# Attention in front of two expert layers: scores and values on four quadrants of TensorE, scores in two PSUM banks, v loaded by even and odd heads

## The chip, the cores and the metric

The kernel runs on one core of one Trainium2 chip. The metric is the device time of one execution in microseconds; before the change the median of two timed runs is 1208.76 us (1208.47 to 1209.05). The profile is one further execution of the same program, recorded by the hardware profiler.

## The reference

Attention inside chunks of 64 tokens, then a gated layer with a root-mean-square norm, then four weighted expert layers, all in float32 (the weights of the gated and the expert layers arrive as float64):

```python
# q, k, v: (4, 8, 576, 64): batch, heads, tokens, head size
q_c, k_c, v_c = (a.reshape(B, H, nc, 64, D) for a in (q, k, v))
scores = np.matmul(q_c, k_c.transpose(0, 1, 2, 4, 3)) / np.sqrt(D)
scores = scores - np.max(scores, axis=-1, keepdims=True)
attn = np.exp(scores)
attn = attn / (np.sum(attn, axis=-1, keepdims=True) + 1e-09)
out = np.matmul(attn, v_c)

x = out.transpose(0, 2, 1, 3).reshape(2304, 512)
xn = x / np.sqrt(np.mean(x * x, axis=-1, keepdims=True) + 1e-06) * rms_g
g = xn @ w_gate                      # 512 x 1536
x = (g / (1 + np.exp(-g)) * (xn @ w_val)) @ w_out

p = probs / (probs.sum(-1, keepdims=True) + 1e-09)
out = sum(p[:, e:e+1] * (np.maximum(x @ w1[e], 0) @ w2[e]) for e in range(4))
```

## The kernel before

The 2304 tokens are cut into 18 tiles of 128 tokens (two chunks of 64) and into five blocks (four of 512 tokens, one of 256). The attention goes tile by tile and fills, for each block, the transposed and normed input of the gated layer in two parts (`xh` and `xl`, the rounded value and what the rounding left). Once a block's tiles are there, the first gate and value units (matmuls `gps` and `vps`, 128x512, line 1170) can run; they are what TensorE has to do beside the attention. Everything after that is large matmuls of 256 or 512 columns.

One tile of the attention, in `attention` (from line 548 on), with the names that the profile shows:

- SP loads q, k and v, each as 128 tokens x 8 heads x 64 (`load_qkv`, line 516; a tile that crosses from one batch to the next takes two DMAs). There are two buffers each for q and k, three for v.
- TensorE transposes q and k, four 128x128 transposes each (`tps`, line 553). ScalarE or VectorE copies them to `qT` and `kT` (lines 562, 564), where 64 rows hold an even head and 64 rows an odd one.
- TensorE computes the scores, 16 products of 64x64 (`sc`, line 583). Head `r` of a pair stands on rows `r * 64` on, and its result goes to the same partitions: rows and result are both `r`. Each product of two float32 operands is two matmuls in the trace, so a tile has 32.
- VectorE takes the maximum and subtracts it (`mx`, line 602; `e`, line 607), ScalarE takes the exponent (line 620; from tile 8 on for two tiles at once).
- TensorE transposes again (`eps`, line 629), an engine copies to `eT` (lines 642, 644), and TensorE multiplies by v, 16 products of 64x65 (`xps`, line 658); the column behind the 64 holds ones, so the row sums come with it. Here both the rows and the result are the chunk `c`.
- VectorE adds up and divides (`den`, `xs`, lines 670 to 676). ScalarE squares (`junk`, line 690), GpSimd takes the root (line 700), GpSimd or VectorE applies the gain (line 707) and ScalarE or VectorE the scale (lines 712, 714).
- TensorE transposes the result (`xtps`, line 723); ScalarE writes `xh` and a plain copy `xf` (lines 731, 744), VectorE writes `xl` (line 736).

PSUM has eight banks: four for the transposes and the scores of the attention (tags `y0` to `y3`, resource "a"), two for the gate and value units (`h0`, `h1`), and one pair of two for the values (tag `av`). When the attention is over, the banks pass to the later stages.

The order of the work on each engine is not written by hand. Class `Plan` is given every step with its engine or engines, an assumed cost, what it needs, which buffers it takes and gives back, and a rank; it lists the steps by the earliest start, walks backwards over the result to set new ranks, repeats this with some random changes up to 120 times and emits the order of the best pass. So a changed cost or a changed number of buffers moves instructions on all engines. Each engine then works through its own queue in order. Line numbers here and in the profile are those of the kernel before.

Of the kernel before, what the change touches and what calls it, by code (L numbers as in the profile page):

```python
# [10 lines left out]
F32 = mybir.dt.float32  # L11
# [4 lines left out]
ALU = mybir.AluOpType  # L16
# [209 lines left out]
def tile_attention_moe_moe2(  # L226
# [135 lines left out]
    plan.buffers("a", [f"y{d}" for d in range(KD)])  # L362
    plan.buffers("av", ["av"])
# [45 lines left out]
    def h_bank(tag, n, name):  # L409
        p = ps_y if tag[0] == "y" else ps_h if tag[1] != "x" else opened()["h"]  # L410
        return p.tile([P, n], F32, tag=tag, name=name)
# [96 lines left out]
    def load_qkv(nm, i):  # L508
        def emit(_, tag):
            src = {"q": q, "k": k, "v": v}[nm]  # L510
            if nm == "v":
                t = v_tiles[tag]
            else:
                t = at_p.tile([P, H, D], F32, tag=tag, name=nm)
# [17 lines left out]
    def attention(grp):  # L532
# [10 lines left out]
        for i in grp:  # L543
# [31 lines left out]
            def scores(_, tag, etag=None, i=i):  # L575
                qT, kT = tiles.pop(("qT", i)), tiles.pop(("kT", i))
                sc = a_bank(tag, [P, HP, 2, CH], "sc")
                for hp in range(HP):
                    for c in range(2):
                        for r in range(2):  # L580
# [3 lines left out]
                                out=sc[rows, hp, c, :], lhsT=qT[rows, hp, cols], rhs=kT[rows, hp, cols],  # L584
                                start=True, stop=True,
                            )
                tiles["sc", i] = sc.rearrange("p a c k -> p (a c) k")
# [3 lines left out]
            s2 = add("PE", 1.2, scores, needs=[cp["q"], cp["k"]], takes=["a"] + (["e"] if i == key else []), rank=rank(i, 16))  # L591
# [8 lines left out]
            def maximum(_, i=i):  # L600
                mx = sm_p.tile([P, H, 1], F32, tag="mx", name="mx")
# [3 lines left out]
            def subtract(_, i=i):  # L605
                o = (i - key) * H
                nc.vector.tensor_tensor(
                    out=tiles["ee", key][:, o:o + H, :], in0=tiles.pop(("sc", i)),
                    in1=tiles.pop(("mx", i)).to_broadcast([P, H, CH]), op=ALU.subtract,
# [4 lines left out]
            sub.gives.append(("a", s2, 0))  # L614
# [9 lines left out]
        for n_, i in enumerate(grp):  # L624
# [25 lines left out]
            def values(_, tag, xtag, i=i):  # L650
                eT, vv = tiles.pop(("eT", i)), tiles.pop(("v", i))
                ps = ps_a.tile([P, 2, 512], F32, tag=tag, name="xps")
                ps = ps[:, :, 0:HP * VW].rearrange("p b (h e) -> p b h e", e=VW)
                for h in range(H):
                    hp, r = h // 2, h % 2
                    for c in range(2):
                        rows = slice(c * CH, (c + 1) * CH)
                        nc.tensor.matmul(  # L658
                            out=ps[rows, h // HP, h % HP, 0:D + 1], lhsT=eT[rows, hp, r * CH:(r + 1) * CH],
                            rhs=vv[rows, h, 0:D + 1], start=True, stop=True,  # L660
                        )
                tiles["xps", i] = ps

            s4 = add("PE", 1.2, values, needs=[ce, first[i]["v"]], takes=["av", "xs"], rank=rank(i, 8))
# [9 lines left out]
            def divide(_, i=i, s4=s4):  # L674
                xs = xs_tiles[s4.ids[1]][:, 0:DM]
                nc.vector.tensor_tensor(
                    out=xs.rearrange("p (b h d) -> p b h d", b=2, h=HP), in0=tiles.pop(("xps", i))[:, :, :, 0:D],
# [1697 lines left out]
```

## Time and profile before

| what | value |
|---|---|
| median of the timed runs | 1208.76 us |
| the profiled execution: span from the first to the last instruction | 1891.7 us |
| mean granted TensorE clock in it | 0.587 |
| TensorE busy (PE) | 1885.1 us |
| VectorE busy (DVE) | 953.0 us |
| ScalarE busy (ACT) | 609.1 us |
| GpSimd busy (POOL) | 251.7 us |
| moved to and from HBM | 235.66 MB |

The profiled execution is much longer than the timed ones. Its span is the only time that is known of it; what lies around the span (the start and the end of an execution) is in no row. The clock column (PEclk) gives the share of full speed (2.4 GHz) that TensorE was granted; its two levels are 1.2 and 2.4 GHz. Engines other than TensorE do not depend on that clock. PEld is TensorE's loading of weights, which overlaps its matmuls. Idle time of an engine that is not the bottleneck costs nothing.

### The profile page before, as it was taken

What the parts mean: (1) busy time and instruction counts of PE and PEld (TensorE: products, weight loads), DVE (VectorE), ACT (ScalarE), POOL (GpSimd) and SP (SyncE); (2) the same over time, 40 slices, a digit from 0 to 9 for tenths busy, and PEclk for the clock granted to TensorE, in tenths of its full rate; (3) what the DMA queues carried; (4) which work ended last, traced back from release to release, by engine and by line L of the source; (5) the groups of instructions that cost most, each with busy time, mean ns of one, the idle gap of its engine ahead of it and who ended that gap; (6) DMA issues with size and microseconds to landing.
All of it is one profiled execution on the core that took longest, in us unless ns stands there. A gap on an engine that the chain in (4) does not pass through costs nothing.

```text
span 1891.7 us, 18628 instructions
## 1 busy us (share of the span) xinstructions
PE 1885.1 (100%) x6962; PEld 1244.2 (66%) x6962; DVE 953.0 (50%) x1407; ACT 609.1 (32%) x957; POOL 251.7 (13%) x198
## 2 busy tenths in 40 slices
PE   9999999999999999999999999999999999999999
PEld 7876666566566665666666666766776666666666
DVE  4655454455456355554545455454656344444455
ACT  5554223332334332323323232232332322222222
POOL 1331110111211001010112112121200011110110
PEclk5555555555555555555555555555666666666666
DMA  8631233324233423333522424243354433534333
GB/s 178 136 69 51 67 112 138 112 85 171 90 139 111 145 89 122 124 132 112 183 105 107 160 96 150 78 150 123 112 178 154 160 130 129 167 138 140 122 111 107
DMA packets 161967, 235.66 MB, mean 125 GB/s; under 512 B 67213, under 2 KB 103125, under 8 KB 161877
## 3 DMA queue, kind: packets, MB, share of 16 engines
q1 hardware_dynamic: 161876, 234.47, 37.7%
q8 instruction: 55, 0.90, 0.2%
q14 instruction: 36, 0.29, 0.0%
HBM read 145.53 MB, written 88.90 MB: 124 GB/s over the span
## 4 chain that ended last, share of the span: by engine, by line
PE 100%; ACT 0%; issue 0%; POOL 0%; DVE 0%; POOLq 0%; ACTq 0%
PE yps L1905 35%; PE hps L1713 25%; PE hps L1316 17%; PE hps L2176 4%; PE yr L2220 4%; PE hps L1445 2%; PE vps L1170 2%; PE gps L1170 2%; PE xps L658 2%; PE tps L553 2%; PE sc L583 2%; PE yo L1523 1%; PE eps L629 1%; PE xtps L723 1%; PE ot L2088 1%; PE warm L2265 0%
## 5 line engine op out<-in xcount | busy, mean ns | idle before, releaser
L1905 PE MATMUL yps<-ha,w 128*128 128x512 f32 x1860 | 667.2, 541 | 0.0
L1905 PEld LDWEIGHTS yps<-ha,w 128*128 128x128 f32 x1860 | 395.9, 215 | 257.2 <-issue 123.1
L1713 PE MATMUL hps<-xa,w 128*128 128x512 f32 x1344 | 479.1, 535 | 0.0
L1713 PEld LDWEIGHTS hps<-xa,w 128*128 128x128 f32 x1344 | 285.6, 215 | 173.6 <-issue 75.2
L1832 DVE TENSOR_TENSOR ha<-hs,ha 128x1024 fp32r<-128x1024 f32 (+1 forms) x126 | 139.5, 1119 | 103.9 <-ACT ha L1826 103.8
L1826 ACT ACTIVATE ha<-hs 128x1024 fp32r<-128x1024 f32 (+1 forms) x126 | 119.0, 959 | 185.6 <-PE yps L1905 140.7
L1937 DVE TENSOR_TENSOR acc<-acc,yps 128x512 f32<-128x512 f32 (+1 forms) x130 | 87.8, 678 | 116.8 <-PE yps L1905 116.4
L1849 POOL TENSOR_TENSOR hs<-hs 128x1024 f32<-128x1024 f32 (+1 forms) x32 | 69.7, 2178 | 517.5 <-DVE ha L1832 487.8
L955 ACT ACTIVATE w<-raw 128x512 fp32r<-128x512 f32 x127 | 77.7, 627 | 120.7 <-PE hps L1713 48.0
L1726 ACT ACTIVATE hps<-hps 128x512 f32<-128x512 f32 x64 | 37.2, 582 | 232.9 <-PE hps L1713 232.9
L1316 PE MATMUL hps<-xh,w 128*128 128x512 f32 x216 | 109.8, 575 | 0.0
L1316 PE MATMUL hps<-xs,w 128*128 128x512 f32 x264 | 106.7, 577 | 0.0
L962 POOL TENSOR_TENSOR w<-raw,w 128x512 fp32r<-128x512 f32 x38 | 52.9, 1394 | 340.6 <-ACT w L955 269.3
L1920 ACT ACTIVATE yps<-yps 128x512 f32<-128x512 f32 x88 | 51.2, 581 | 118.0 <-PE yps L1905 116.2
L1774 DVE SCALAR_TENSOR_TENSOR hs<-hps,pb 128x512 f32<-128x512 f32 x96 | 65.5, 687 | 42.5 <-PE hps L1713 42.4
L1316 PEld LDWEIGHTS hps<-xs,w 128*128 128x128 f32 x264 | 58.0, 220 | 43.5 <-issue 24.6
L962 DVE TENSOR_TENSOR w<-raw,w 128x512 fp32r<-128x512 f32 x89 | 65.2, 754 | 36.6 <-ACT w L955 36.4
L1734 DVE TENSOR_TENSOR hps<-hps,p 128x512 f32<-128x512 f32 x32 | 22.4, 699 | 116.3 <-ACT hps L1726 116.3
L1832 DVE TENSOR_TENSOR ha<-hl,ha 128x1024 fp32r<-128x1024 f32 x42 | 50.8, 1224 | 52.2 <-ACT ha L1826 52.2
L2220 PEld LDWEIGHTS yr<-w,hb 128*128 128x128 f32 x384 | 72.7, 259 | 5.2 <-issue 2.3
L2176 PE MATMUL hps<-xh,w 128*128 128x256 f32 x256 | 75.1, 374 | 0.0
L2220 PE MATMUL yr<-w,hb 128*128 128x256 f32 x384 | 74.1, 373 | 0.0
(175 smaller groups left out, 2126.4 us busy)
## 6 DMA issues: line engine op xcount, KB each, us to landing
w<-wk SPq DMA_DIRECT2D x126, 512.0 KB, 4.1
wk<-w SPq DMA_DIRECT2D x111, 512.0 KB, 3.0
raw<-in_moe_w_dram SPq DMA_DIRECT2D x33, 512.0 KB, 4.6
hl<-sd SPq DMA_DIRECT2D x48, 256.0 KB, 3.1
sd<-s SPq DMA_DIRECT2D x38, 256.0 KB, 2.2
w<-wk SPq DMA_DIRECT2D x32, 256.0 KB, 2.9
wk<-w SPq DMA_DIRECT2D x29, 256.0 KB, 2.0
raw<-in_moe_w_gate_dram SPq DMA_DIRECT2D x12, 512.0 KB, 3.7
```

The costliest lines, as they stand in the source:

```text
L955: nc.scalar.activation(out=w1t[key, c][:, :, 0], in_=half(c in "DA"), func=AF.Copy)
L962: e_.tensor_tensor(out=w[:, :, 1], in0=half(c in "DA"), in1=f32(w[:, :, 0]), op=ALU.subtract)
L1170: nc.tensor.matmul(out=banks[u], lhsT=w[:, wi, kk, :], rhs=x[j][:, kk, 0:n], start=(kk, p) == (0, 0), stop=(kk, p) == (KD - 1, 2),)
L1316: nc.tensor.matmul(out=bank[b], lhsT=w[:, m, wi, kk, :], rhs=xx[xi][:, kk, :], start=start and (kk, i) == (0, 0), stop=(kk, i) == (1, 2), ...
L1713: nc.tensor.matmul(out=bank[b], lhsT=w[:, m, wi, kk, :], rhs=xx[xi][:, kk, :], start=start and (kk, i) == (0, 0), stop=(kk, i) == (1, 2), ...
L1826: nc.scalar.activation(out=ops[tg, g][m][0][:, cuts[k]], in_=x(frm, k), func=AF.Copy)
L1832: nc.vector.tensor_tensor(out=l[:, cuts[k]], in0=x(frm, k), in1=f32(h[:, cuts[k]]), op=ALU.subtract)
L1849: e_.tensor_tensor(out=x(to, k), in0=x(one, k), in1=x(two, k), op=op)
L1905: nc.tensor.matmul(out=bank[b, d][:, cols], lhsT=w[:, m, wi, d, :], rhs=hh[xi][:, fp, cols], start=start and (fp, i) == (0, 0), stop=(fp, ...
L1937: nc.vector.tensor_tensor(out=a[:, cols], in0=a[:, cols], in1=bank[b, d][:, cols], op=ALU.subtract if minus else ALU.add)
L2176: nc.tensor.matmul(out=got["b"], lhsT=w[:, m, wi, kk, :], rhs=(xh, xl)[xi][REST][:, 2 * m + kk, 0:n], start=(m, kk, k) == (0, 0, 0), stop= ...
L2220: nc.tensor.matmul(out=got["y"][:, d * 2 * P:(d + 1) * 2 * P], lhsT=hs[2 * g + f // 2][:, f % 2, xi, t * P:(t + 1) * P], rhs=w[:, f % 2, w ...
```

## The change

Scores and values now use all four 64x64 quadrants of TensorE's array: a head or key half `r` on the rows, and the chunk `c` on the columns, so the result of chunk `c` stands on partitions `c * 64` on. Two row halves that write the same partitions write to different PSUM banks: the scores of even heads go to one bank, of odd heads to another. So the scores now take a pair of banks, as the values do. There are two such pairs (`av0`, `av1`), and two banks instead of four are left for transposes (`y0`, `y1`). For the values, the rows of v must hold even heads on the lower 64 partitions and odd heads on the upper ones, so a tile of v is loaded by four DMAs (two chunks, two halves of the heads) of 64 partitions each. VectorE's steps follow the new layout of the scores and of the values. The assumed cost of scores and values goes from 1.2 to 0.6.

```diff
-    plan.buffers("a", [f"y{d}" for d in range(KD)])
-    plan.buffers("av", ["av"])
+    plan.buffers("a", ["y0", "y1"])
+    plan.buffers("av", ["av0", "av1"])
...
     def h_bank(tag, n, name):
-        p = ps_y if tag[0] == "y" else ps_h if tag[1] != "x" else opened()["h"]
+        p = ps_y if tag in ("y0", "y1") else ps_h if tag in ("h0", "h1") else opened()["h"]
...
             if nm == "v":
                 t = v_tiles[tag]
-            else:
-                t = at_p.tile([P, H, D], F32, tag=tag, name=nm)
+                for off, n, b, s in runs(i * P, P):
+                    for c in range(n // CH):
+                        for r in range(2):
+                            nc.sync.dma_start(
+                                out=t[r * CH:(r + 1) * CH, off // CH + c, :, 0:D],
+                                in_=src[b, r::2, s + c * CH:s + (c + 1) * CH, :].rearrange("h p d -> p h d"),
+                            )
+                tiles[nm, i] = t
+                return
+            t = at_p.tile([P, H, D], F32, tag=tag, name=nm)
...
-                sc = a_bank(tag, [P, HP, 2, CH], "sc")
+                sc = ps_a.tile([P, 2, 512], F32, tag=tag, name="sc")
+                sc = sc[:, :, 0:HP * CH].rearrange("p r (h k) -> p r h k", k=CH)
                 for hp in range(HP):
                     for c in range(2):
                         for r in range(2):
                             rows = slice(r * CH, (r + 1) * CH)
                             cols = slice(c * CH, (c + 1) * CH)
                             nc.tensor.matmul(
-                                out=sc[rows, hp, c, :], lhsT=qT[rows, hp, cols], rhs=kT[rows, hp, cols],
+                                out=sc[cols, r, hp, :], lhsT=qT[rows, hp, cols], rhs=kT[rows, hp, cols],
                                 start=True, stop=True,
                             )
...
-            s2 = add("PE", 1.2, scores, needs=[cp["q"], cp["k"]], takes=["a"] + (["e"] if i == key else []), rank=rank(i, 16))
+            s2 = add("PE", 0.6, scores, needs=[cp["q"], cp["k"]], takes=["av"] + (["e"] if i == key else []), rank=rank(i, 16))
...
-                    out=tiles["ee", key][:, o:o + H, :], in0=tiles.pop(("sc", i)),
-                    in1=tiles.pop(("mx", i)).to_broadcast([P, H, CH]), op=ALU.subtract,
+                    out=tiles["ee", key][:, o:o + H, :].rearrange("p (h r) k -> p r h k", r=2),
+                    in0=tiles.pop(("sc", i)), in1=tiles.pop(("mx", i)).to_broadcast([P, 2, HP, CH]), op=ALU.subtract,
...
-                ps = ps[:, :, 0:HP * VW].rearrange("p b (h e) -> p b h e", e=VW)
-                for h in range(H):
-                    hp, r = h // 2, h % 2
+                ps = ps[:, :, 0:HP * VW].rearrange("p r (h e) -> p r h e", e=VW)
+                for hp in range(HP):
                     for c in range(2):
-                        rows = slice(c * CH, (c + 1) * CH)
-                        nc.tensor.matmul(
-                            out=ps[rows, h // HP, h % HP, 0:D + 1], lhsT=eT[rows, hp, r * CH:(r + 1) * CH],
-                            rhs=vv[rows, h, 0:D + 1], start=True, stop=True,
-                        )
+                        for r in range(2):
+                            rows = slice(r * CH, (r + 1) * CH)
+                            cols = slice(c * CH, (c + 1) * CH)
+                            nc.tensor.matmul(
+                                out=ps[cols, r, hp, 0:D + 1], lhsT=eT[rows, hp, cols],
+                                rhs=vv[rows, c, hp, 0:D + 1], start=True, stop=True,
+                            )
...
-            s4 = add("PE", 1.2, values, needs=[ce, first[i]["v"]], takes=["av", "xs"], rank=rank(i, 8))
+            s4 = add("PE", 0.6, values, needs=[ce, first[i]["v"]], takes=["av", "xs"], rank=rank(i, 8))
...
-                    out=xs.rearrange("p (b h d) -> p b h d", b=2, h=HP), in0=tiles.pop(("xps", i))[:, :, :, 0:D],
+                    out=xs.rearrange("p (h r d) -> p r h d", r=2, h=HP), in0=tiles.pop(("xps", i))[:, :, :, 0:D],
```

The planner's new order shows on every engine; the last 4181 of TensorE's 6388 instructions stand as before, while on the engines beside it steps trade places, and some change between VectorE, ScalarE and GpSimd, up to the last few dozen instructions. On TensorE, before, where the first gate unit comes in between the tiles of the attention (a product of two float32 operands counts once here, so a set of scores is x16):

```order
L583 MATMUL sc<-kT,qT 64x64 x16
L629 MATMUL eps<-ident,e 128x128 x4
L553 MATMUL tps<-ident,q 128x128 x4
L553 MATMUL tps<-ident,k 128x128 x4
L1170 MATMUL gps<-xh_93,w 128x512
L1170 MATMUL gps<-xl_98,w 128x512
L1170 MATMUL gps<-xh_93,w 128x512 x2
L1170 MATMUL gps<-xl_98,w 128x512
L1170 MATMUL gps<-xh_93,w 128x512
L723 MATMUL xtps<-ident,xs 128x128 x4
```

On TensorE, after the change, at the same place (lines have moved by nine or ten):

```order
L592 MATMUL sc<-kT,qT 64x64 x16
L561 MATMUL tps<-ident,q 128x128 x4
L1180 MATMUL gps<-xh_93,w 128x512
L1180 MATMUL gps<-xl_98,w 128x512
L1180 MATMUL gps<-xh_93,w 128x512 x2
L1180 MATMUL gps<-xl_98,w 128x512
L1180 MATMUL gps<-xh_93,w 128x512
L638 MATMUL eps<-ident,e 128x128 x4
L561 MATMUL tps<-ident,k 128x128 x4
```

With two banks, k's transposes no longer follow q's; gate matmuls and the transposes of e stand between them.

On SP, which issues the loads, before, where the loads of the first weights (`raw`) come in between those of the tiles:

```order
L516 DMA q<-in_q_dram 128x8x64
L779 DMA raw<-in_moe_w_gate_dram 128x4x256
L516 DMA k<-in_k_dram 128x8x64
L516 DMA v<-in_v_dram 128x8x64
L516 DMA q<-in_q_dram 128x8x64
L779 DMA raw<-in_moe_w_val_dram 128x4x256
L516 DMA k<-in_k_dram 128x8x64
L516 DMA v<-in_v_dram 64x8x64 x2
```

On SP, after the change, in the same stretch:

```order
L789 DMA raw<-in_moe_w_val_dram 128x4x256
L524 DMA q<-in_q_dram 128x8x64
L516 DMA v<-in_v_dram 64x4x64 x8
L789 DMA raw<-in_moe_w_gate_dram 128x4x256
L524 DMA k<-in_k_dram 128x8x64
L516 DMA v<-in_v_dram 64x4x64 x8
L524 DMA q<-in_q_dram 128x8x64
```

Each tile of v is four DMAs instead of one or two, here for two tiles in a row (x8), and a load of k or q stands behind them. In all there are 72 loads of v instead of 20.

## Rows read from the trace of the kernel before

**Rows 1.** The cores: span, and mean granted TensorE clock.

```profile
core 0: 1891.7 us, clock 0.587
```

**Rows 2.** The page: busy time by engine, and the granted clock in 40 slices.

```profile
PE 1885.1 (100%) x6962; PEld 1244.2 (66%) x6962; DVE 953.0 (50%) x1407; ACT 609.1 (32%) x957; POOL 251.7 (13%) x198
...
PEclk5555555555555555555555555555666666666666
```

**Rows 3.** Busy time by stage: stretch, length, engines, granted clock, DMA share, GB/s.

```profile
core 0: us, PE busy (x) PEld busy (x) DVE busy (x) ACT busy (x) POOL busy (x), PEclk, DMA share, GB/s
0.00:130.00 130.00, 127.17 (x1349) 100.66 (x1350) 70.93 (x132) 68.06 (x124) 34.04 (x44) 0.57 0.63 137
130.00:300.00 170.00, 170.00 (x619) 108.77 (x618) 85.98 (x146) 62.49 (x107) 30.66 (x30) 0.56 0.25 86
300.00:1302.00 1002.00, 1002.00 (x3075) 648.63 (x3074) 501.58 (x738) 316.82 (x492) 135.05 (x95) 0.56 0.35 121
```

**Rows 4.** The chain of waits, 47 to 53 us: start, us, what.

```profile
47.34 0.71 PE xtps L723 x4
48.05 1.67 PE xps L658 x32
49.72 0.86 PE eps L629 x4
50.58 1.66 PE sc L583 x32
52.24 0.86 PE xtps L723 x4
```

**Rows 5.** The first scores of one block: stretch, length, matmuls and weight loads under way.

```profile
43.95:43.95 0.01, 0.01 (x2) 0.01 (x2) 0.56 0.00 0
43.96:44.05 0.09, 0.09 (x2) 0.09 (x4) 0.56 0.00 0
44.05:44.06 0.01, 0.01 (x4) 0.01 (x5) 0.56 0.00 0
44.06:44.11 0.05, 0.05 (x4) 0.05 (x6) 0.56 0.00 0
44.11:44.12 0.01, 0.01 (x6) 0.01 (x5) 0.56 0.00 0
```

**Rows 6.** Groups by line, VectorE, 0 to 260 us: division and subtraction.

```profile
L676 DVE TENSOR_TENSOR xs<-xps,den 128x512 f32<-128x512 f32 x18 | 12.4, 690 | 0.6
L607 DVE TENSOR_TENSOR e<-sc,mx 128x512 f32<-128x512 f32 x18 | 12.4, 687 | 0.6
```

**Rows 7.** The timeline, 28.6 to 34 us: transposes and their last evictions.

```profile
28.63 0.93 PE L553 MATMUL tps<-ident,q 128*128 128x128 f32 x4
...
29.31 0.96 PE L553 MATMUL tps<-ident,k 128*128 128x128 f32 x4
...
29.66 0.60 ACT L562 ACTIVATE qT<-tps 128x512 f32<-128x512 f32 x1 [1.38 <-PE tps L553]
...
30.11 0.97 PE L629 MATMUL eps<-ident,e 128*128 128x128 f32 x4
...
30.38 0.69 DVE L564 COPY kT<-tps 128x512 f32<-128x512 f32 x1 [0.15 <-PE tps L553]
...
30.92 0.87 PE L723 MATMUL xtps<-ident,xs 128*128 128x128 f32 x4
...
31.11 0.60 ACT L642 ACTIVATE eT<-eps 128x512 f32<-128x512 f32 x1 [0.24 <-PE eps L629]
...
33.23 0.69 DVE L736 TENSOR_TENSOR xl<-xtps,xh 128x512 fp32r<-128x512 f32 x1 [1.77 <-ACT xf L744]
```

**Rows 8.** SP: the loads of v (duration min/median/max), and what its queue waited for.

```profile
L516 SPq DMA_DIRECT2D v<-in_v_dram x20: 367/588/2750, 7.2 to 133.2; - x20
...
SPq L516 <- PE tps L553: 46.7, 21, 6.6
SPq L516 <- PE xps L658: 19.9, 4, 9.8
```

More of the change, by code (lines that the diff above doesn't have):

```diff
@@ L583, in scores @@
                             nc.tensor.matmul(
-                                out=sc[rows, hp, c, :], lhsT=qT[rows, hp, cols], rhs=kT[rows, hp, cols],
+                                out=sc[cols, r, hp, :], lhsT=qT[rows, hp, cols], rhs=kT[rows, hp, cols],
                                 start=True, stop=True,
                             )
-                tiles["sc", i] = sc.rearrange("p a c k -> p (a c) k")
+                tiles["sc", i] = sc
                 if i == key:
                     tiles["ee", i] = at_p.tile([P, ng * H, CH], F32, tag=etag, name="e")
-            s2 = add("PE", 1.2, scores, needs=[cp["q"], cp["k"]], takes=["a"] + (["e"] if i == key else []), rank=rank(i, 16))
+            s2 = add("PE", 0.6, scores, needs=[cp["q"], cp["k"]], takes=["av"] + (["e"] if i == key else []), rank=rank(i, 16))
             s2.gives += [("qT", norm["q", i], 1), ("kT", norm["k", i], 1)]
@@ L600, in maximum @@
             def maximum(_, i=i):
-                mx = sm_p.tile([P, H, 1], F32, tag="mx", name="mx")
+                mx = sm_p.tile([P, 2, HP, 1], F32, tag="mx", name="mx")
                 nc.vector.tensor_reduce(out=mx, in_=tiles["sc", i], axis=AX.X, op=ALU.max)
@@ L613, in attention @@
             sub = add("DVE", 0.69, subtract, needs=[m], rank=rank(i, 14))
-            sub.gives.append(("a", s2, 0))
+            sub.gives.append(("av", s2, 0))
             subs.append(sub)
@@ L2255, in tile_attention_moe_moe2 @@
         for i in range(3):
-            t = v_tiles[f"v_{i}"] = at_p.tile([P, H, VW], F32, tag=f"v_{i}", name="v")
-            nc.gpsimd.memset(t[:, :, D:VW], 1.0)
+            t = v_tiles[f"v_{i}"] = at_p.tile([P, 2, HP, VW], F32, tag=f"v_{i}", name="v")
+            nc.gpsimd.memset(t[:, :, :, D:VW], 1.0)
         for i in range(2):
```

## The prediction

> **What bounds the kernel now.** I read the cores first [rows 1], then the page's busy times and clock row [rows 2], the busy times by stage [rows 3], the chain of waits in a settled part of the attention [rows 4], single matmuls in it [rows 5], and last the evictions, transposes and loads that the change touches [rows 6 to 8].
>
> The profiled execution has a span of 1891.7 us, and the timed ones have a median of 1208.76 us. The rows show why these differ: in the profile TensorE was granted 0.587 of full speed on the mean [rows 1], nearer to its lower level (1.2 GHz) than to its upper (2.4 GHz), and was busy for 1885.1 of the 1891.7 us [rows 2]. At full clock that is about 0.587 x 1891.7 = 1110 us of TensorE work. A timed run of 1208.76 us must therefore have had at least 1110 / 1208.76 = 0.92 of the clock. The other engines' busy times do not hang on TensorE's clock. So a stage that reads as "PE 100%" here may belong to another engine in a timed run, and each stage has to be worked out again: TensorE's busy time times its clock, beside the others as they stand.
>
> For the attention, 0 to 130 us [rows 3], that gives TensorE 127.2 x 0.57 = 72.5 us, VectorE 70.9, ScalarE 68.1, and the DMA engines a busy share of 0.63 x 130 = 81.9. Four resources need nearly the same, and TensorE is not the largest. For 130 to 300 us it gives TensorE 170 x 0.56 = 95.2 against VectorE 86.0, and for 300 to 1302 us 561 against 501.6: there TensorE leads. The change touches only the first stage.
>
> **The change part by part.** Sum, in the profile's own time: one block of scores takes 1.66 us and one of values 1.67 [rows 4]. There are 18 of each: 18 x (1.66 + 1.67) = 59.9 us. In these blocks matmuls begin two at a time: two are in flight until 44.05, four from there, six from 44.11 [rows 5]. The code writes only the quadrants (0,0) and (1,1), so two quadrants work beside each other. After the change every quadruple of instructions goes to four quadrants. If those work as independently as the two do, a block takes half: 59.9 / 2 = 29.9 us less TensorE time, 1.6% of the span. At the clock of that stage this is 29.9 x 0.56 = 16.8 us at full clock, and at the 0.92 of the timed runs 16.8 / 0.92 = 18.2 us. The number of matmuls and loads is unchanged. Bounds: nothing, if the two new quadrants do not overlap, and 16.8 to 18.2 us, if TensorE bounds the stage throughout.
>
> What of that lies on the path? With 16.8 us taken off, TensorE needs 72.5 - 16.8 = 55.7 us in a stage where VectorE needs 70.9, ScalarE 68.1 and the DMA engines 81.9. Nothing of what these three do gets less. What remains is that a tile's work passes from engine to engine, and each tile spends less time in its scores and values before the next engine may start. Between 0 and 16.8 I take a third, 5.6 us: nearer to zero, since three resources each need more than TensorE will. TensorE's tail of the program is ordered as before (its last 4181 of 6388 instructions); on the engines beside it steps trade places there, which may go either way by a few us and is left to the range.
>
> The maximum, the subtraction and the division keep their 512 elements. Subtraction now writes pieces of 64 elements, and both read two banks. The division before already reads pieces from two banks and takes 690 ns, the plain subtraction 687 [rows 6]: 36 x 3 ns is 0.1 us. I take zero.
>
> Four banks for transposes become two. A tile has four sets of transposes, each holding a bank until its last eviction ends [rows 7]: q from 28.63 to 29.66 + 0.60 = 1.63 us, k from 29.31 to 31.07 = 1.76, e from 30.11 to 31.71 = 1.60, x from 30.92 to 33.92 = 3.00. That is 7.99 us per tile, over two banks 4.0 us, over 18 tiles 71.9 us. In a timed run the four transposes of a set are quicker (about 0.80 us here, 0.80 x 0.56 = 0.45 there), so 7.99 - 4 x 0.35 = 6.6 us, 59 us in all. That fits beside the 81.9 of the DMA engines, so I cost it at nothing. The cover is gone once evictions wait longer (third rival). The order shows the planner living with it: k's transposes no longer follow q's directly but stand behind gate matmuls.
>
> Loads of v go from 20 to 72 on SP. A v issue takes 0.367 to 2.750 us, median 0.588 [rows 8]. 52 more are 52 x 0.367 = 19.1 us at the minimum and 30.6 us at the median. SP's queue is in order, and the loads of q and k behind v in it are delayed by 3 x 0.37 to 3 x 0.59, or 1.1 to 1.8 us per tile. What hides this is that SP waits for TensorE to free q and k buffers: 46.7 us, and 19.9 us for v's [rows 8]. That cover is 66.6 us in the profile and less in a timed run. Bounds 0 to 30.6 us. I take zero, since the cover is more than twice the median cost.
>
> Sum: -5.6 us, 1208.76 - 5.6 = 1203 us.
>
> A rule of the Trainium skill speaks against the change and is weighed here. In the trace, four weight loads are already under way while the first two matmuls run, before the second pair begins [rows 5], and before the change there are only two quadrants that those loads can go to. So a load runs beside the matmul of its own row group. "TensorE: Matmul & The Clock Gate", Part 3 (the mechanism), says that a weight load overlaps matmuls in flight only when the row groups differ. By that rule the two quadrants of one row half would take turns after the change, a block would not get shorter, and the sum would be 1208.8. The trace does not bear the rule out here, so it gets a small share of the second rival.
>
> **The rivals.**
>
> First: TensorE bounds the attention in timed runs too, because its clock there is not full (0.92 is only the mean). For it: no other engine is seen to hold TensorE in the profile, where its idle time in 130 us is 2.8 us [rows 3]. Against it: at 0.92 TensorE needs 72.5 / 0.92 = 78.8 us, still under the 81.9 of DMA. Time: 1208.8 - 17 or 18 = 1191.
>
> Second: nothing comes of it, because the stage ends with loads and evictions, or because four quadrants do not overlap (the rule above). For it: DMA's 81.9 is the largest need of the stage. Against it: DMA's share counts packets in flight, and goes over what moves. Time: 1208.
>
> Third, slower: two banks. The mechanism is TensorE's in-order queue. The first transpose of a set waits for an eviction, and behind it stand scores, values and gate matmuls that could run; VectorE and ScalarE then wait for those. Without any wait the banks need 59 us of the stage's 81.9. It decides once a set holds its bank longer by (81.9 x 2 / 18 - 6.6) / 4 = 0.6 us, which is one instruction of VectorE (0.69) in front of each eviction. With two in front, 1.38 us, a tile needs 6.6 + 4 x 1.38 = 12.1 us, the stage 18 x 12.1 / 2 = 109 us, 27 us more than 81.9. Between one (3 us) and two (27 us) I price it at 12 us: 1221. For it: VectorE and ScalarE are nearly full in this stage. Against it: two banks of their own now serve scores and values, which took turns with the transposes before.
>
> **How the numbers follow.** The forecast (a part of the saving, 1196 to 1207) gets 0.45, TensorE-bound (about 1191) 0.25, nothing (about 1208) 0.15, slower by the banks or by SP (about 1221) 0.15. The time is that of the likeliest, 1203. For 8 in 10 the range takes in most of the first rival and the nearer half of the third: 1189 to 1217. A change of over 2% is 24 us, about what a measurement of this kernel can tell from none. Faster by that means under 1184.6, more than the whole saving of 18.2 us: 0.05. Slower by that means over 1232.9, reached only with nearly two instructions in front of every eviction, or with all 30.6 us of SP showing: 0.04. Within: 0.91.
>
> **What would show it.** In the changed kernel's chain of waits a block of 32 scores or values should read about 0.83 us at a granted clock of 0.56 (0.47 us at full clock) instead of 1.66, with matmuls beginning four at a time. If it reads 1.6, the second rival's quadrants are right. VectorE's and ScalarE's busy times in the attention should be as before. TensorE's idle time should grow there, ended by evictions if the third rival is right, and by loads if SP is late. If the profile is taken at a low clock again, its span should shrink by up to 1.6%, and by more of it than the timed runs show; timed runs that shrink by as much would mean that the stage was TensorE's after all.

## The result, and the profile after

The changed kernel takes 1223.62 us (median; 1223.49 to 1223.76) against 1208.76. The ratio is 1.0121, 95% interval 1.0091 to 1.0150: slower by 1.2%, or about 14.6 us, where 1203 was forecast and the range ended at 1217.

The profile shown ahead of the prediction had a granted clock of 0.587 [rows 1]. The kernel before was profiled again (run before_again) and was then granted 0.999 (1.000 is full speed), as every later profile was granted 0.987 or more; it is this second profile that the one after can be laid beside. The page of before, profiled again (busy time, clock in 40 slices):

```profile
PE 1194.0 (99%) x6962; PEld 1015.3 (84%) x6962; DVE 956.1 (79%) x1407; ACT 601.6 (50%) x957; POOL 248.9 (21%) x198
```

and of the changed kernel:

```profile
PE 1186.1 (97%) x6962; PEld 1003.8 (82%) x6962; DVE 963.1 (79%) x1411; ACT 603.8 (49%) x960; POOL 240.0 (20%) x191
...
PEclk9899899999999999999999999999999999999999
```

TensorE is busy for 7.9 us less, yet the span went from 1208.5 to 1221.6 us: 21 us of idle time came in. VectorE's and ScalarE's busy times are as before within 1%. The clock row dips in its second and fifth slice only (a slice is 30.5 us, so both lie in the first 153 us). By stretches of 20 us, the kernel before (columns as in [rows 3]):

```profile
0.00:20.00 20.00, 15.09 (x223) 13.38 (x224) 6.45 (x11) 8.67 (x15) 1.27 (x14) 1.00 0.99 184
20.00:40.00 20.00, 16.69 (x278) 14.02 (x277) 14.68 (x30) 14.56 (x28) 6.48 (x7) 0.91 0.93 211
40.00:60.00 20.00, 18.10 (x319) 15.72 (x319) 18.01 (x35) 15.82 (x30) 8.48 (x9) 1.00 0.91 195
60.00:80.00 20.00, 19.83 (x297) 17.06 (x294) 18.16 (x33) 15.74 (x31) 9.22 (x9) 1.00 0.98 208
80.00:100.00 20.00, 20.00 (x298) 17.40 (x297) 17.04 (x34) 17.21 (x29) 11.22 (x10) 1.00 0.51 106
...
120.00:140.00 20.00, 20.00 (x105) 17.09 (x104) 18.45 (x22) 11.82 (x16) 2.63 (x3) 1.00 0.14 54
...
0.00:140.00 140.00, 129.71 (x1682) 111.21 (x1683) 111.68 (x193) 98.13 (x172) 50.38 (x60) 0.99 0.68 150
```

and the changed one:

```profile
0.00:20.00 20.00, 14.52 (x227) 12.51 (x228) 6.92 (x12) 8.60 (x15) 1.28 (x14) 1.00 0.83 167
20.00:40.00 20.00, 11.28 (x201) 9.19 (x200) 13.46 (x26) 11.49 (x21) 0.90 (x2) 0.83 0.92 200
40.00:60.00 20.00, 12.20 (x309) 9.71 (x307) 17.43 (x35) 15.54 (x32) 9.73 (x10) 1.00 0.81 169
60.00:80.00 20.00, 17.12 (x264) 13.93 (x265) 11.87 (x25) 12.42 (x22) 6.78 (x7) 0.91 0.77 164
80.00:100.00 20.00, 18.78 (x281) 15.32 (x280) 17.57 (x31) 16.43 (x31) 10.22 (x8) 1.00 0.78 162
...
120.00:140.00 20.00, 15.29 (x90) 11.64 (x89) 17.68 (x30) 12.19 (x22) 8.03 (x7) 0.84 0.27 90
...
0.00:140.00 140.00, 108.94 (x1612) 88.16 (x1613) 102.20 (x188) 92.91 (x168) 44.24 (x55) 0.94 0.68 150
```

The difference lies in the first 140 us. In these TensorE did 129.7 x 0.99 = 128.4 us of full-clock work before and 108.9 x 0.94 = 102.4 now. The change takes 15.1 us of work away (below), so 128.4 - 15.1 - 102.4 = 10.9 us are late at 140 us, most of the 13.1 us by which the spans differ. Two things read differently as well: the loads moved 164 to 200 GB/s in the first 80 us, where they moved 184 to 211 before, and go on at 162 GB/s from 80 to 100 us; and a new hole of 4.7 us, with a lower clock, opens at 120 to 140 us.

The blocks themselves got shorter nearly as forecast. From the chain of waits, before profiled again:

```profile
71.61 1.08 PE sc L583 x32
...
73.71 1.08 PE xps L658 x32
```

and after:

```profile
67.66 0.63 PE xps L668 x32
...
78.98 0.69 PE sc L592 x32
```

18 x (1.08 + 1.08 - 0.69 - 0.63) = 15.1 us less TensorE work, where 16.8 was forecast. Two sizes behind that were off and nearly cancel: a block went to 0.6 of its time, not to half, and at full clock it took 1.08 us before, not 1.66 x 0.56 = 0.93.

What TensorE waits for in the first 140 us (us in total, times, longest) was, before:

```profile
PE tps L553 <- DMA k<-in_k_dram: 3.4, 4, 1.7
PE tps L553 <- ACT e L620: 2.4, 1, 2.4
```

and after:

```profile
PE xtps L733 <- ACT xs L722: 9.7, 3, 7.4
PE tps L561 <- DVE raw L817: 5.1, 1, 5.1
...
PE tps L561 <- DMA q<-in_q_dram: 2.5, 2, 1.6
PE gps L1180 <- DVE xl L746: 2.1, 1, 2.1
PE tps L561 <- DMA k<-in_k_dram: 1.9, 3, 0.9
```

The largest, xtps behind xs (9.7 us), is a place in TensorE's order: transposes of x stand ahead of work that could run. The 5.1 us are put down to a conversion of VectorE (`raw`), which writes nothing that the transposes of q read; the trace shows what they waited for. The load of q that SP issued at 55.54 us told of its landing at 61.96 us, and the transposes began at 62.10. In SP's queue that load stood behind eight quarter loads of v, which took SP 6.25 us from 48.55 us on. So the waits for loads of q and k come to 2.5 + 1.9 + 5.1 = 9.5 us, where before had 3.4 and, by the same reading, the 2.4 us put down to `e`.

### The profile page after: what moved, and what is told of

It is laid out like the page before. It is cut to its first block, busy times and chain, and to the rows that moved or that the text cites. A ratio compares the mean times of both kernels' runs of the same rounds, so it can differ in the third digit from the quotient of the medians.

```text
span 1221.6 us, 18708 instructions
## 1 busy us (share of the span) xinstructions
PE 1186.1 (97%) x6962; PEld 1003.8 (82%) x6962; DVE 963.1 (79%) x1411; ACT 603.8 (49%) x960; POOL 240.0 (20%) x191
## 4 chain that ended last, share of the span: by engine, by line
PE 92%; DVE 3%; DMA 2%; ACT 1%; issue 1%; POOL 0%; SPq 0%; DVEq 0%; POOLq 0%; ACTq 0%
PE yps L1915 34%; PE hps L1723 25%; PE hps L1326 15%; PE yr L2230 4%; PE hps L2186 4%; PE hps L1455 2%; PE gps L1180 2%; PE yo L1533 1%; PE tps L561 1%; PE vps L1180 1%; PE xps L668 1%; DMA k<-in_k_dram 1%; PE sc L592 1%; DMA g_bc<-in_moe_rms_g_dram 1%; PE ot L2098 1%
## 5 line engine op out<-in xcount | busy, mean ns | idle before, releaser
L1915 PE MATMUL yps<-ha,w 128*128 128x512 f32 x1860 | 425.9, 388 | 0.0
L1915 PEld LDWEIGHTS yps<-ha,w 128*128 128x128 f32 x1860 | 346.3, 188 | 70.4
L1723 PE MATMUL hps<-xa,w 128*128 128x512 f32 x1344 | 313.2, 390 | 0.0
L1723 PEld LDWEIGHTS hps<-xa,w 128*128 128x128 f32 x1344 | 250.2, 188 | 50.7 <-DVE p L1747 0.2
L1326 PE MATMUL hps<-xh,w 128*128 128x512 f32 x232 | 77.5, 389 | 0.0
L1326 PE MATMUL hps<-xs,w 128*128 128x512 f32 x264 | 65.3, 390 | 0.1
L1326 PEld LDWEIGHTS hps<-xs,w 128*128 128x128 f32 x264 | 49.3, 188 | 10.9 <-ACT hps L1340 0.5
L979 DVE TENSOR_TENSOR raw<-raw 128x256 f32<-128x256 f32 x113 | 48.0, 425 | 12.9 <-POOL w L972 7.7
L1836 ACT ACTIVATE ha<-hl 128x1024 fp32r<-128x1024 f32 x42 | 43.7, 1056 | 21.7 <-PE yps L1915 11.7
L1326 PEld LDWEIGHTS hps<-xh,w 128*128 128x128 f32 x232 | 43.6, 188 | 8.9
```

Source lines behind the costliest of these rows:

```text
L1326: nc.tensor.matmul(out=bank[b], lhsT=w[:, m, wi, kk, :], rhs=xx[xi][:, kk, :], start=start and (kk, i) == (0, 0), stop=(kk, i) == (1, 2), ...
L1723: nc.tensor.matmul(out=bank[b], lhsT=w[:, m, wi, kk, :], rhs=xx[xi][:, kk, :], start=start and (kk, i) == (0, 0), stop=(kk, i) == (1, 2), ...
L1836: nc.scalar.activation(out=ops[tg, g][m][0][:, cuts[k]], in_=x(frm, k), func=AF.Copy)
L1915: nc.tensor.matmul(out=bank[b, d][:, cols], lhsT=w[:, m, wi, d, :], rhs=hh[xi][:, fp, cols], start=start and (fp, i) == (0, 0), stop=(fp, ...
```

## The experiments

The change has four parts that can be taken apart: the banks, the quadrants, v's four loads a tile, and the 0.6 us (for 1.2) at which scores and values are booked in the planner, which sets the order of all engines. The theory after the result: the quadrants gain what was forecast, and v's loads or the new order cost more. The rival: the two banks (third rival of the prediction). A third idea was a single load, g_bc (the gain row), that the new order issues late. Ratios are to the kernel before, with their 95% intervals.

**First batch** (the kernel before beside it: 1209.64 us).

before_again asks which engine bounded the attention at full clock:

> The kernel before, unchanged, for a profile at the clock of the timed runs. If TensorE has about 10 us of idle time in its attention here (its work at full clock, some 1195 us, is nearly the whole span), TensorE bounded that stage after all and the four-quadrant saving was there to be had. If it idles 20 us or more, other engines bounded it as the prediction said. Time 1208 to 1210.

1210.3 us. TensorE's idle time in the first 140 us is 140 - 129.7 = 10.3 us, the first case of the expectation: TensorE bounded that stage, and the saving was there to be had. c12_v_one, below, shows how much of it.

v_one, against the changed kernel (it leaves out v's new layout, so it does the same work but doesn't compute the reference):

```diff
-                    for c in range(n // CH):
-                        for r in range(2):
-                            nc.sync.dma_start(
-                                out=t[r * CH:(r + 1) * CH, off // CH + c, :, 0:D],
...
+                    nc.sync.dma_start(
+                        out=t.rearrange("p c h e -> p (c h) e")[off:off + n, :, 0:D],
+                        in_=src[b, :, s:s + n, :].rearrange("h p d -> p h d"),
+                    )
```

> The changed kernel with its order kept, but v loaded by one or two DMAs per tile in the old layout, so that the values multiply rows of v that belong to other heads (the amount of work is the same, the output is not the reference's). SP theory: the four loads of v take 2.6 to 3.5 us of SP's queue per tile in place of 0.6, and q, k and the gain row wait behind them; without them the time falls to 1193 to 1204. Bank theory: two banks for transposes hold TensorE; the time stays at 1217 to 1224.

1216.16 us, ratio 1.0052 [1.0037, 1.0067]. That lies between the ranges of the two theories. The four loads cost about 0.7%, somewhat over half of the loss; the rest stays with v loaded whole.

g_early, the changed kernel with g_bc's load issued right behind the third load of k:

> The changed kernel with the load of the gain row issued right behind the k of the third tile, all else in the same order. In the changed kernel TensorE waits 7.4 us for the first scaled tile, behind that load. If that wait is a loss of its own, the time falls by 5 to 8 us, to 1216 to 1219. If SP's queue holds the stage anyway (SP theory), the wait only moves to the next load: 1220 to 1224.

1223.86 us, 1.0118 [1.0103, 1.0133]: no gain. One late load is not the cause.

b_banks, the kernel before with the changed one's banks:

```diff
-    plan.buffers("a", [f"y{d}" for d in range(KD)])
-    plan.buffers("av", ["av"])
+    plan.buffers("a", ["y0", "y1"])
+    plan.buffers("av", ["av0", "av1"])
...
-            s2 = add("PE", 1.2, scores, needs=[cp["q"], cp["k"]], takes=["a"] + ...
+            s2 = add("PE", 1.2, scores, needs=[cp["q"], cp["k"]], takes=["av"] + ...
```

> The kernel before with only its banks changed: two for transposes, two pairs for scores and values, scores on two quadrants as before, v in one or two DMAs; the planner orders it anew. Bank theory: slower than before by 8 us or more, 1217 or above. SP theory: within 4 us of before, 1205 to 1213.

1213.14 us, 1.0024 [1.0008, 1.0041]. The banks, with the order that the planner makes for them, cost some 3 us, a fifth of the loss, and not the 8 us or more of the bank theory. How much of the 3 us is the banks' and how much the draw of a new order is not shown: c12 and c12_seed6, below, differ by 0.18% in nothing but the draw.

**Second batch** (before: 1208.6 us): the changed kernel with the booking put back,

```diff
-            s2 = add("PE", 0.6, scores, ...
+            s2 = add("PE", 1.2, scores, ...
...
-            s4 = add("PE", 0.6, values, ...
+            s4 = add("PE", 1.2, values, ...
```

with v in four loads (c12), and with v_one's edit as well (c12_v_one).

> The changed kernel with the planner told 1.2 for scores and values as before, so that its order is that of b_banks, and v in one or two DMAs in the old layout (the values multiply rows of v of other heads; the work is the same). Against b_banks (1213.1) only the four quadrants are new. If TensorE bounds the attention, all of the 16 us shows: 1197 to 1200. If loads and VectorE bound it, as the prediction said, little shows: 1206 to 1213.

1206.02 us, 0.9974 [0.9962, 0.9986]: faster than the kernel before, but like v_one it doesn't compute the reference. The order on every engine is that of b_banks, so the step from there is the quadrants (with VectorE's new layout) alone: -0.50%, or -6 us. The first 140 us of b_banks and of c12_v_one:

```profile
0.00:140.00 140.00, 130.56 (x1665) 110.22 (x1666) 107.40 (x192) 102.85 (x181) 40.71 (x54) 0.98 0.69 152
```

```profile
0.00:140.00 140.00, 124.83 (x1705) 100.72 (x1706) 113.25 (x199) 106.92 (x188) 42.07 (x55) 0.95 0.71 159
```

With shorter blocks TensorE's idle time rises from 9.4 to 15.2 us and its granted clock falls from 0.98 to 0.95: part of the 15.1 us goes into waiting for others and into the clock.

> The changed kernel with the planner told 1.2 for scores and values, v in four DMAs as in the change. Against c12_v_one only the loads of v differ. SP theory: they cost 7 us or more here too, 1208 to 1222, c12_v_one plus 7 to 12. If the cost of the loads hung on the planner's order for 0.6, the two differ by less than 3 us.

1215.02 us, 1.0043 [1.0026, 1.0060]. The four loads cost 0.69% here too (from c12_v_one), and the booking 0.78% (from c12 to the changed kernel). The first of these shows in what TensorE waits for in the first 140 us. In c12:

```profile
PE tps L561 <- DMA k<-in_k_dram: 4.8, 4, 2.4
PE tps L561 <- DMA q<-in_q_dram: 4.5, 3, 2.5
```

and in c12_v_one, with the same order:

```profile
PE tps L559 <- DMA k<-in_k_dram: 2.0, 1, 2.0
```

One more wait in each (3.3 and 2.0 us) is put down to another engine, but there too the load had landed 0.14 us before the transposes began, as in the others. With these it is 12.6 us against 4.0: 8.6 us more, beside 8.3 us of time. The changed kernel has 9.5 us of such waits and v_one 0.8. With seed 6 (fourth batch) the waits at 0.6 differ by as much, those at 1.2 only by about 4 us.

> The changed kernel with its order, v in one or two DMAs in the old layout, and the gain row loaded behind the third k. In v_one TensorE still waits 6.7 us for the first scaled tile behind the gain row. If that wait is what is left of the loss, the time falls by 5 to 8 us below v_one (1216.2): 1208 to 1211. If the planner's order for 0.6 is the loss (end of the attention, where TensorE idles 4.7 us between 120 and 140 us in every run with that order), it stays at 1214 to 1217.

1217.71 us, 1.0074 [1.0059, 1.0089]. A null again.

c12_v_act is c12 with the loads of r = 1 issued from ScalarE's queue:

```diff
-                            nc.sync.dma_start(
+                            (nc.scalar if r else nc.sync).dma_start(
```

> c12 with two of the four loads of v of a tile issued from ScalarE's queue. SP theory: half of v's time on SP is gone, so it lies between c12 and c12_v_one, 3 to 6 us under c12, unless ScalarE's own work is held up by the issues (then no faster than c12).

1213.94 us, 1.0039 [1.0024, 1.0054]: not told apart from c12. With half of the issues off SP, TensorE's waits for the loads of q and k fall from 9.3 to 2.5 us by the same view, yet most of the price of the four loads stays; where it went is not shown.

**Third batch** (before: 1209.52 us): is the 0.6 order slow because the planner doesn't know what the loads cost on SP, or by the luck of its random search?

v28 and c12_v28 change the booking of v's load in the changed kernel and in c12:

```diff
-                ld[nm] = add("SP", 1.3, load_qkv(nm, i), ...
+                ld[nm] = add("SP", 2.8 if nm == "v" else 1.3, load_qkv(nm, i), ...
```

> The changed kernel with one number of its planner altered: a tile's v load is booked on SP with 2.8 us instead of 1.3, about what its four transfers take there in the changed kernel's trace (2.58 to 3.55 us). Instructions are the same, only their order can move. Theory A (the order planned with 0.6 is slow because the planner takes SP for free where the four loads hold it): an order that knows their price wins back most of the 9 us that the step from cost 1.2 to 0.6 took: 1213 to 1217 us. Theory B (the order is slow for a reason other than the loads; the same 0.78% stood between the two orders with v loaded whole): 1220 to 1226 us, no gain. Theory C (each replanning is a fresh draw of some us either way): anything from 1212 to 1228.

1218.58 us, 1.0079 [1.0064, 1.0094].

> As the run before, but with scores and values booked at 1.2 us as in the kernel before (the order c12 was planned with, 1215.0 us). Theory A: with SP's price known the order brings loads forward and takes back 3 to 6 us of the 8 that the four loads cost: 1209 to 1212. Theory B: the loads' cost is SP's issuing itself and no order helps: 1213 to 1217. Theory C (a fresh draw): 1208 to 1225.

1217.42 us, 1.0067 [1.0051, 1.0084]. The true price helps the 0.6 order by 0.4%, less than theory A had; the 0.2% that it costs the 1.2 order is little more than another seed alone does (0.18%, c12_seed6). Neither gives back what the loads cost.

seed6, the changed kernel with `SEED = 6` for 5:

> The changed kernel with the start of the planner's random search changed from 5 to 6, all costs as in the changed kernel (0.6; v load 1.3). Theory A (cost 0.6 makes slow orders, since it tells the planner of TensorE room that the loads and VectorE don't give): about as slow, 1220 to 1226. Theory C (the 9 us between the 1.2 and the 0.6 order is a draw): it may land anywhere, and as the one draw seen was bad, more likely below than above: 1212 to 1222.

1224.37 us, 1.0123 [1.0108, 1.0139]. The same as with seed 5: no sign of bad luck in the draw.

c12_v_pool issues all four from GpSimd (`nc.gpsimd` for `nc.sync` in the loads of v):

> The kernel planned with 1.2 (c12, 1215.0 us) with all four v transfers of a tile issued from GpSimd's queue instead of SP's. GpSimd is busy a fifth of the span. Theory A (the four loads cost by SP's issuing, 8 us): with SP as free as in the kernel before the time comes near that of the loads in one piece (1206.0): 1206 to 1210. Theory B (their cost is the transfers themselves, packets of 256 bytes in twice four pieces, whichever queue issues them): 1213 to 1217. Issuing from ScalarE for half of them took only 1 us off, which speaks for B or for a cost on ScalarE; GpSimd has more room. A third way: GpSimd's issue holds up its own work (the gains and the roots in the attention's chain) and the time is above 1217.

1222.71 us, 1.0110 [1.0095, 1.0125]: the third way of its expectation, GpSimd's own work held up. ScalarE's waits for GpSimd's root (`rinv`) in the first 140 us, in c12:

```profile
ACT xs L722 <- POOL rinv L710: 3.7, 4, 2.0
```

and in c12_v_pool:

```profile
ACT xs L722 <- POOL rinv L710: 12.2, 8, 3.0
```

What one issue of v takes on its engine (duration ns min/median/max, first and last start) in the changed kernel:

```profile
L516 SPq DMA_DIRECT2D v<-in_v_dram x72: 595/608/2635, 7.4 to 111.4; - x72
```

in c12_v_act:

```profile
L516 ACTq DMA_DIRECT2D v<-in_v_dram x36: 602/620/2043, 6.1 to 105.0; - x36
L516 SPq DMA_DIRECT2D v<-in_v_dram x36: 595/615/3126, 6.7 to 105.0; - x36
```

and in c12_v_pool:

```profile
L516 POOL DMA_DIRECT2D v<-in_v_dram x72: 615/616/776, 1.7 to 113.8; - x72
```

An issue of a quarter tile (64 KB) takes 0.6 us on whichever engine does it. 72 of them are 44 us of GpSimd. Moving them did not remove the price. That the transfers themselves are dearer (theory B) is not what the traces show: in the first 140 us the kernel before moved 21.02 MB in 64121 packets, 58848 of them under 512 bytes, and the changed one 21.02 MB in 65188, 59664 of them under 512.

**Fourth batch** (before: 1210.07 us): both bookings drawn again with v loaded whole, and the 0.6 order run with the long blocks.

> Quadrants, v loaded by one or two transfers a tile (its rows stand as in the kernel before, so values meet other heads' rows), scores and values booked at 1.2 us, and the planner's search started from 6 instead of 5. With seed 5 this was 1206.0 us (0.9974). Theory S (booking 0.6 makes slow orders whatever the draw, 1.2 good ones): 1204 to 1209. Theory D (orders differ by draw, and 1206 was a lucky one): anywhere from 1204 to 1218, likely over 1209.

1207.12 us, 0.9980 [0.9968, 0.9992].

> As the run before, but booked at 0.6 (with seed 5: 1216.2 us, 1.0052). Theory S: 1213 to 1219 again. Theory D: anywhere from 1204 to 1218, likely under 1213.

1217.25 us, 1.0060 [1.0042, 1.0078].

b_banks06 is b_banks with 0.6 for 1.2 in both bookings:

> The kernel before with the banks of the changed one (b_banks, two-quadrant blocks of 1.1 us, 1213.1 us) but with its planner told 0.6, so that TensorE, ScalarE and SP follow the order of the kernel with quadrants and v loaded whole (1216.2 us). If that order is slow in itself, by about 9 us whichever blocks run in it: 1220 to 1224, with the idle time of 120 to 140 us in it again. If it is slow only because short blocks leave gaps in it: 1212 to 1216, since the long blocks fill them.

1227.44 us, 1.0141 [1.0125, 1.0156].

> Quadrants with v in four loads from SP, booked at 1.2, the search started from 6 (with seed 5: 1215.0 us, 1.0043). Theory S: 1212 to 1217. Theory D: 1208 to 1226. A time below 1208 would be a kernel with the quadrants that beats the one before.

1217.07 us, 1.0061 [1.0045, 1.0077].

Theory S holds: with either seed the orders booked at 0.6 are slower than those at 1.2. b_banks06 shows that the order is slow in itself, with the long blocks too. All ratios to the kernel before, side by side:

| blocks | v | booked 1.2: seed 5, 6 | booked 0.6: seed 5, 6 |
|---|---|---|---|
| two quadrants | whole | 1.0024 | 1.0141 |
| four | whole | 0.9974, 0.9980 | 1.0052, 1.0060 |
| four | four loads | 1.0043, 1.0061 | 1.0121, 1.0123 |

Down from the first row to the second the quadrants gain 0.50% or 0.89%; from the second to the third the loads cost 0.63 to 0.81%; to the right the booking costs 0.62 to 0.80% with short blocks and 1.17% with long ones.

Where the 0.6 orders lose it, by stretches; c12_v_one (1.2):

```profile
20.00:40.00 20.00, 15.36 (x282) 12.14 (x283) 14.99 (x29) 15.00 (x31) 6.69 (x7) 0.84 0.91 202
...
120.00:140.00 20.00, 20.00 (x110) 17.20 (x110) 19.35 (x23) 14.13 (x20) 4.32 (x4) 1.00 0.21 72
```

v_one (0.6), the same work:

```profile
20.00:40.00 20.00, 11.70 (x200) 9.55 (x200) 13.99 (x25) 10.69 (x20) 0.55 (x1) 0.67 1.09 229
...
120.00:140.00 20.00, 15.29 (x59) 11.66 (x58) 16.77 (x21) 10.85 (x16) 4.10 (x4) 0.83 0.25 78
```

Both are short of TensorE work in the same two places as the changed kernel, though v_one's loads run at 229 GB/s there. b_banks06 has them too, with 11.82 and 15.41 us busy; its idle time in the first 140 us is 19.9 us, where b_banks, the same work, has 9.4. The first place in the timeline of v_one:

```profile
30.97 1.29 DVE L715 TENSOR_TENSOR xs<-xs,g_bc 128x512 f32<-128x512 f32 x2 [0.98 <-DMA g_bc<-in_moe_rms_g_dram]
31.76 1.33 ACT L720 ACTIVATE xs<-xs,rinv 128x512 f32<-128x512 f32 x2 [4.14 <-DVE xs L715]
...
32.54 1.97 PE L731 MATMUL xtps<-ident,xs 128*128 128x128 f32 x8 [6.68 <-ACT xs L720]
...
39.26 1.06 PE L559 MATMUL tps<-ident,k 128*128 128x128 f32 x4
```

TensorE stands at the x transposes of two tiles for 6.68 us until VectorE has multiplied by g_bc, and at the lowered clock (0.50 there) the transposes after it take 1.06 us a set, where a set takes 0.60 to 0.66 at full clock. c12_v_one has no TensorE wait above 2.0 us between 18 and 62 us. Bringing g_bc forward shortened the wait to 5.6 us (v_one_g_early) and the time not at all. That the order is slow is shown; why a planner that is told less than 1.2 makes such orders is not. One reading, not tested: it counts neither the clock that falls in the gap nor loads that come late.

**Fifth batch** (before: 1209.49 us): can some of the 6 us be kept with v in one load? scores4 starts from b_banks and puts only the scores on four quadrants. The head on a partition half depends on the half, and values take their columns to match:

```diff
-                                out=sc[rows, hp, c, :], lhsT=qT[rows, hp, cols], ...
+                                out=sc[(r ^ c) * CH:((r ^ c) + 1) * CH, c, hp, :], lhsT=qT[rows, hp, cols], ...
...
-                            out=ps[rows, h // HP, h % HP, 0:D + 1], lhsT=eT[rows, hp, r * CH:(r + 1) * CH],
+                            out=ps[rows, h // HP, h % HP, 0:D + 1], lhsT=eT[rows, hp, (r ^ c) * CH:((r ^ c) + 1) * CH],
```

> The kernel before with the banks of the changed one, v in one load, values on two quadrants as before, and only the scores on four quadrants (output half r^c, bank c; values take their columns to match), planned with 1.2 for both. By the runs so far: banks +0.24%, half of the quadrants' -0.50%: ratio 0.9999, 1209 us, no difference from before. If the quadrants' gain needs both blocks short it stays at b_banks's 1.0024 (1212); if the short scores block alone frees TensorE where it is waited for (the chain tps, scores, maximum), 0.9974 (1206).

1208.40 us, 0.9996 [0.9988, 1.0005].

> The same with the planner's search started from 6. With values and scores on quadrants the two seeds gave 0.9974 and 0.9980; so the same as scores4 within 0.2%: 1206 to 1212 us.

1208.08 us, 0.9991 [0.9982, 1.0000]. The timeline of scores4 has the two kinds of block side by side:

```profile
95.24 0.63 PE L584 MATMUL sc<-kT,qT 64*64 64x64 f32 x30
...
99.67 1.15 PE L659 MATMUL xps<-v,eT 64*64 64x65 f32 x32
```

The table foretold 0.9999; half of the gain about pays for the banks. No kernel that computes the reference was clearly faster than the one before.

## Why the prediction was wrong

**The quadrants** saved nearly the TensorE work that was forecast, 15.1 us for 16.8, and 6 us of time (b_banks to c12_v_one) for the 5.6. That the 5.6 came so near is partly luck. It is a third of the saving, a share that no row gave; its reason, that three others each need more than TensorE, does not hold (the clock, below); and in the order booked at 0.6 the same step is worth 0.89%, or 11 us (b_banks06 to v_one). What holds of it is that the freed time goes in part into waits for others. The second rival's doubt falls: a block went from 1.08 to 0.63 or 0.69 us. The prediction read the rule of "TensorE: Matmul & The Clock Gate", Part 3 (the mechanism), in the Trainium skill, that a weight load overlaps matmuls in flight only when the row groups differ, as the two quadrants of a row half taking turns; these rows do not agree with that.

**The loads of v** are the first step that failed: "I take zero, since the cover is more than twice the median cost." They cost 0.69% (c12_v_one to c12), 8.3 us. The price on SP was about right: 52 more issues of 0.608 us are 31.6 us, for the 30.6 at the median. The cover was not there. SP's waits for the transposes in the first 140 us of before, profiled again, are 11.3 us where [rows 8] had 46.7:

```profile
SPq L516 <- PE tps L553: 11.3, 9, 2.3
```

SP's queue in the same trace:

```profile
23.00 0.80 SPq L516 DMA_DIRECT2D v<-in_v_dram  x1
23.90 2.06 SPq L516 DMA_DIRECT2D q<-in_q_dram  x1
...
27.60 2.62 SPq L516 DMA_DIRECT2D v<-in_v_dram  x2
30.32 2.36 SPq L516 DMA_DIRECT2D q<-in_q_dram  x1
32.78 1.28 SPq L516 DMA_DIRECT2D k<-in_k_dram  x1
```

and after:

```profile
28.57 0.43 SPq L789 DMA_DIRECT2D raw<-in_moe_w_val_dram  x1
29.11 0.44 SPq L524 DMA_DIRECT2D q<-in_q_dram  x1
29.59 7.09 SPq L516 DMA_DIRECT2D v<-in_v_dram  x8
36.78 0.55 SPq L789 DMA_DIRECT2D raw<-in_moe_w_gate_dram  x1
37.43 1.46 SPq L524 DMA_DIRECT2D k<-in_k_dram  x1
```

At full clock SP issues one load after another in both kernels, and hardly waits for TensorE in between. The 46.7 us of waits for q and k buffers [rows 8] belong to a TensorE at 0.57 of its clock. The cover was read from a profile in which TensorE was the late one, and the prediction said itself that it would be "less in a timed run" without working out how much less. Before, the DMA engines are nearly full (share 0.91 to 0.99 in the first 80 us) and an issue often lasts 2 us; after, two tiles of v hold SP for 7.09 us, k's load waits behind them, and the share falls to 0.77 to 0.81 from 40 to 80 us. TensorE then stands for q and k: the 8.6 us of c12 over c12_v_one.

**The order** is the second. The prediction let the reordering "go either way by a few us" and left it to the range. It costs 0.78%, 9.4 us (c12 to the changed kernel), and 0.62 to 0.80% over both seeds and ways of loading v: as much as the loads, and more than "a few us". The edit from 1.2 to 0.6 looked like bookkeeping; 0.6 is also nearer to the true 0.63 to 0.69. It was never asked what the new order makes TensorE stand at.

**The banks** were costed at nothing; they cost 0.24%, 3 us, with their replanning. The third rival gave 12 us for them or for SP: its time, 1221, came nearest, but by luck of the sum: loads and order made it, not transposes that wait for evictions.

The steps from the kernel before to the changed one, in per cent: banks +0.24, quadrants -0.50, loads +0.69, booking +0.78, together +1.21. They are a chain (before, b_banks, c12_v_one, c12, changed kernel), so they add up to the measured +1.21 by the way they are made; that speaks for no step by itself. What does is the table: each step was measured in other company too, and the quadrants' depends on it most (0.50 or 0.89).

**The clock.** Both steps rest on one more. The prediction took TensorE's need in the first 130 us as busy time times clock, 127.2 x 0.57 = 72.5 us, and the clock of the timed runs as 0.92, where the later profile has 0.999. At a granted clock of 0.98, TensorE was busy for 85 us over the same matmuls (the first 1350, up to 95.30 us in before_again, with 10.3 us idle), more than the prediction's 81.9 of the DMA engines; a block of scores took 1.08 us for 1.66, a factor of 0.65 and not 0.56. So "TensorE is not the largest" was wrong, and slack was looked for on the wrong engines: with TensorE busy for 129.7 of the first 140 us, what makes it stand costs time.

## What to carry to other kernels

Work out an operand's new layout as loads before counting the matmuls that it saves: here four issues of 0.6 us took the place of one and cost 0.63 to 0.81%, about what the four quadrants gave (0.50 or 0.89%). A number that only a planner reads is an edit of the whole order; compare its orders by what the in-order engine will stand at, and test the number by itself. And before cover is read from a profile, see whether the engine that gives it ran at the clock of the timed runs.

## What the runs showed of the hardware

- The same kernel was granted 0.587 in one profile [rows 1] and 0.999 in the next, with timed medians of 1208.76 and 1209.64 us; the other engines' busy times agree within 1.3%. TensorE was 100% busy in the first, so idle time was not what lowered its clock there. A block of scores took 1.66 us at 0.56 [rows 4] and 1.08 at full clock.
- In the later profiles the clock was lowered where TensorE had idle time: in v_one it was 0.67 of full speed from 20 to 40 us with 11.70 us busy (at the lower level, 1.2 GHz, from 26.69 to 40.34), and 0.83 from 120 to 140 us with 15.29. Not every gap did so in its own stretch: the changed kernel had 12.20 us busy from 40 to 60 us at 1.00, and 0.91 in the next 20 us. Of the 26 us of full-clock work by which the two kernels differ in the first 140 us, about a fifth (108.9 x 0.05 = 5 us) is clock; the rest is work taken away and idle time.
- All four 64x64 quadrants worked beside each other in float32: 32 matmuls in 0.63 or 0.69 us at full clock, where two quadrants took 1.08.
- A DMA issue of 64 KB on 64 partitions takes as long (0.6 us at the least) on SP, ScalarE and GpSimd, while a whole tile of 256 KB on 128 partitions took 0.37 us at the least [rows 8]; the four half tiles of 128 KB on 64 partitions in that row took 0.60 at the least.
